# A recurrent-memory kernel: half of a streamed weight chunk made resident, paid for by a single output-tail buffer and a new schedule for the tail's heads

## Chip, cores, metric

One core of one Trainium2 chip. The metric is the device time of one execution in microseconds (us). The views of the profile name the engines PE (TensorE; PEld are its weight loads), DVE (VectorE), ACT (ScalarE), POOL (GpSimd) and SP (SyncE).

## The reference, cut to what matters

The program computes two unrelated things and lays them side by side. Part A (a long convolution by FFT) takes the first 470 us or so and the change does not touch it. Part B is a recurrence over 64 segments of 32 rows:

```python
mem = mem0                                     # 8 rows
for s in range(64):
    h = concat([mem, x[32 * s:32 * s + 32]])   # 40 rows
    q, k, v = h @ Wq, h @ Wk, h @ Wv           # 1024 -> 32 heads x 128 each
    p = softmax(where(mask, q @ k.T * scale, -1e9))
    o = (p @ v) @ Wo                           # 4096 -> 1024
    mem = o[:8]                                # the next segment needs this
    outs.append(o[8:])
```

`Wq`, `Wk`, `Wv` and `Wo` are 32 MB in bfloat16, and every segment needs all of them. They do not all fit on chip.

## The kernel before

The weights are 64 chunks of [128, 2048] bfloat16, 512 KB each. 43 stay on chip; 21 are streamed. Two of the streamed ones are kept in free accumulator columns after segment 0 ("kept"), so each segment loads 19 chunks from HBM through a ring of six slots. A slot is refilled when TensorE has used its chunk:

```python
STREAM = (0, 1, 3, 7, 11, 15, 21, 23, 25, 29, 33, 36, 40, 43, 46, 49, 51, 53, 59, 60, 62)
KEPT = {18: "A", 6: "B"}          # order_s[18] is place 59, order_s[6] is place 21
RING = 6

def fetch():                       # the next load, into a slot that has come free
    if loads:
        s, ch = loads.pop(0)
        live[s, ch] = k, t = slot()
        nc.sync.dma_start(t[:], stream_src(ch))

def done(ch):                      # after the last matmul that reads this chunk
    if ch in streamed:
        ...
        free.append(live.pop((now[0], ch))[0])
        ...
        if nxt in kept and s > 0:
            unkeep(s, kept[nxt])   # the freed slot takes the kept chunk back: no load here
        else:
            fetch()
```

A segment's places are: 0-7 K projection of head group 0 (`k0`), 8-15 Q, 16-23 K and 24-31 Q of group 1, 32-47 V, 48-63 the output projection (`out_proj`, two heads a chunk).

32 rows per segment (24 new ones and the 8 memory rows) go through the main path. The last 8 rows of a segment, the *tail*, have their attention computed there too, but their output projection is gathered over a pair of segments: `OTB` holds the tail's attention outputs of both, and the class `Tail` multiplies them by `Wo` head by head, 32 heads per pair. I call the first segment of a pair *even* (`j == 0`) and the second *odd*.

```python
class Tail:
    def __init__(self, OTB, b, acc=None):
        ...
        nc.vector.memset(self.acc, 0.0)            # columns of the accumulator tile SB
    def head(self, h, w): ...                      # 4 small matmuls; the 32nd calls store()
    def run(self, n): ...                          # n heads whose Wo chunk is resident
    def store(self):
        YB = one.tile([128, 256], BF, tag="QT", name="YB")   # QT0, QT1 and OT use this buffer too
        nc.vector.tensor_copy(YB[:], self.acc)
        for dq in range(4):
            nc.gpsimd.dma_start(<8 output rows of both segments>, YB[32 * dq:32 * dq + W, :])

# one segment, cut
k0 = Proj(0, 0).run().evac()
q0 = Proj(1, 0).run(4); KT0 = keys(0); last_queries(0); ...
k1 = Proj(0, 1).run(4)
QT0 = one.tile([128, 4, 4, 32], BF, tag="QT", name="QT")
nc.vector.tensor_copy(QT0[:], transposes(q0))
k1 = k1.run(4).evac()
scores(0, QT0, KT0)
...
out_proj(range(0, 5), OT0); attend(1, PT1, V1); OT1 = evac_o(1)
out_proj(range(5, 8), OT0)
out_proj(range(8, 16), OT1)        # tail heads of streamed chunks run inside, INLINE says in which segment
Y = one.tile([128, 256], BF, tag="PT", name="Y")
nc.scalar.copy(Y[:], yacc[:, 0:256])
if j == NB - 1 and not last:
    tail = Tail(OTB, b)
if tail is not None and not last:
    tail.run(TURN[0])              # 6 heads while ScalarE copies Y
if not last:
    fill_mem(pend[s + 1][0], Y)    # transposes of Y into the next segment's input
nc.gpsimd.dma_start(<output rows of segment s>, Y[:])
if tail is not None and not last:
    tail.run(TURN[1])              # 4 heads while VectorE copies the memory rows
```

The last lines are the *turn*: the next segment cannot start before the memory rows have gone from `Y` into its input.

Of the kernel before, what the change touches and what calls it, by code (L numbers as in the profile page):

```python
# [9 lines left out]
BF = mybir.dt.bfloat16  # L10
F32 = mybir.dt.float32
# [11 lines left out]
KEPT = {18: "A", 6: "B"}  # L23
TURN = (6, 4)
INLINE = {1: 0, 3: 1, 5: 0, 11: 1, 12: 0, 14: 1}
N2, N3 = 12, 19
# [358 lines left out]
def b_kernel(ctx: ExitStack, tc, x, mem0, Wq, Wk, Wv, Wo, outb, n_seg, run_a):  # L385
    nc = tc.nc
    SEG = 32
    NX = 24
    NB = 2
# [9 lines left out]
    order = []  # L399
# [7 lines left out]
    streamed = set()  # L407
# [4 lines left out]
    own = {mg: [ch for ch in resident if ch[0] < 3 and (ch[0], ch[2]) == mg] for mg in groups}  # L412
# [8 lines left out]
    def dram_chunk(ch):  # L421
        m, a, g = ch
        return Wo_v[a] if m == 3 else W_v[m][a, g]
# [4 lines left out]
    def stream_src(ch):  # L428
        return WS[ring_order.index(ch), :, 0:2048]
# [186 lines left out]
    one = ctx.enter_context(tc.tile_pool(name="b_one", bufs=1, side="right", reuse_waits="tile"))  # L616
    two = ctx.enter_context(tc.tile_pool(name="b_two", bufs=2, side="right", reuse_waits="tile"))
    ps_acc = ctx.enter_context(tc.tile_pool(name="b_ps_acc", bufs=2, space=PSUM))
# [15 lines left out]
    tacc = SB[:, 200:456]  # L634
# [14 lines left out]
    def slot():  # L649
        k = free.pop(0)  # L650
        t = ring.tile([128, 2048], BF, tag=f"wring{k}", name="wring")
        return k, t

    def fetch():
        if loads:
            s, ch = loads.pop(0)
            live[s, ch] = k, t = slot()
            nc.sync.dma_start(t[:], stream_src(ch))

# [12 lines left out]
    def pieces(ch):  # L672
        if ch in res:
            return [(0, 2048, res[ch])]
        t = live[now[0], ch][1]
        if kept.get(ch) == "B" and now[0] > 0:
            return [(0, 768, WB[:]), (768, 2048, t[:, 768:2048])]
        return [(0, 2048, t[:])]
# [7 lines left out]
    def done(ch):  # L686
        if ch in streamed:
# [7 lines left out]
            else:  # L695
                fetch()

    P_pad = one.tile([128, 5, 64], BF, name="P_pad")
    nc.vector.memset(P_pad[:], 0.0)

# [17 lines left out]
    with tc.manual_schedule():  # L718
# [17 lines left out]
        class Tail:  # L736


            def __init__(self, OTB, b, acc=None):
                self.OTB, self.b, self.acc = OTB, b, tacc if acc is None else acc  # L740
                self.seeded = acc is None
                self.left = list(range(32))
                nc.vector.memset(self.acc, 0.0)  # L743

            def head(self, h, w):
                g, c, i = h // 16, (h % 16) // 4, h % 4
                first = len(self.left) == 32
                self.left.remove(h)
                for dq in range(4):
                    o = (h % 2) * 1024 + dq * 256  # L750
                    for x, y, r in columns(w, o, o + 256):
                        nc.tensor.matmul(self.acc[32 * dq:32 * dq + W, x - o:y - o],  # L752
                                         lhsT=self.OTB[:, c, 4 * g + i, :], rhs=r,
                                         start=first and not self.seeded, stop=not self.left,
                                         skip_group_check=True, tile_position=(0, 32 * dq))
                if not self.left:
                    self.store()
# [12 lines left out]

        OTB = tail = own = None
        for s in range(n_seg):
# [60 lines left out]

            def softmax_a():
                mx = two.tile([128, 5], F32, tag="mx", name="mx")
                nc.vector.tensor_reduce(out=mx[:], in_=S, op=ALU.max, axis=AX.X)  # L836
                nc.vector.tensor_tensor(out=S, in0=S, in1=mx[:].unsqueeze(2).to_broadcast([128, 5, 40]),
                                        op=ALU.subtract)
                nc.scalar.activation(S, S, ACT.Exp, scale=scale)

            def softmax_b():
                ssum = two.tile([128, 5], F32, tag="ssum", name="ssum")
                nc.vector.tensor_reduce(out=ssum[:], in_=S, op=ALU.add, axis=AX.X)  # L843
# [38 lines left out]
            def out_proj(hps, OT):  # L882
                for hp in hps:
                    ch = (3, hp, 0)
                    w = pieces(ch)
                    for hh in range(2):
                        h = 2 * hp + hh
                        g, c, i = h // 16, (h % 16) // 4, h % 4
                        for dq in range(4):
                            o = hh * 1024 + dq * 256  # L890
                            for x, y, r in columns(w, o, o + 256):
                                nc.tensor.matmul(yacc[32 * dq:32 * dq + 32, x - o:y - o], lhsT=OT[:, c, i, :],  # L892
                                                 rhs=r, start=(h == 0 and x == o), stop=(h == 31),
                                                 tile_position=(0, 32 * dq))
                    if tail is not None and 2 * hp in tail.left and (ch in streamed or last):
                        if last or INLINE[hp] == j:
                            tail.head(2 * hp, w)
                            tail.head(2 * hp + 1, w)
                    if own is not None and ch in streamed:
                        own.head(2 * hp, w)  # L900
                        own.head(2 * hp + 1, w)
                    done(ch)

            k0 = Proj(0, 0).run().evac()
            q0 = Proj(1, 0).run(4)
# [8 lines left out]
            scores(0, QT0, KT0)  # L914
            softmax_a()
            q1 = Proj(1, 1).run(4)
            KT1 = keys(1)
            last_queries(1)
            nc.scalar.copy(KT1[:, :, :, 0:32], transposes(k1))
            PT0 = softmax_b()  # L920
            q1 = q1.run(4).evac()
# [4 lines left out]
            scores(1, QT1, KT1)  # L926
            softmax_a()
            pv1 = Proj(2, 1).run(4)
            if j == 0:
                OTB_new = one.tile([128, 4, 8, 8 * NB], BF, tag=f"OTB{b % 2}", name="OTB")  # L930
                OTB = OTB_new
            attend(0, PT0, V0)
            OT0 = evac_o(0)
            PT1 = softmax_b()
            pv1.run(4)
# [3 lines left out]
            yacc = ps_acc.tile([128, 512], F32, tag="acc", name="yacc")  # L939
            if last:  # L940
                own = Tail(OTB, b, ps_acc.tile([128, 512], F32, tag="acc", name="own_acc")[:, 0:256])
            out_proj(range(0, 5), OT0)
# [5 lines left out]
            nc.scalar.copy(Y[:], yacc[:, 0:256])  # L948
            if j == NB - 1 and not last:
                tail = Tail(OTB, b)  # L950
            if tail is not None and not last:
                tail.run(TURN[0])
            if not last:
                fill_mem(pend[s + 1][0], Y)
            nc.gpsimd.dma_start(bass.AP(outb.tensor, outb.offset + SEG * s * 2048, [[256, 4], [2048, 32], [1, 256]]), Y[:])
            if tail is not None and not last:
                tail.run(TURN[1])
            if last:
                own.run(32)

# [69 lines left out]
```

## Time and profile before

Median 2198.11 us of 3 runs (2195.46 to 2198.48). What matters:

| read from | value |
|---|---|
| pair of segments, from the copies of the memory rows | 53.63 us (even 26.31, odd 27.37) |
| lost DMA time per pair | 0.63 us |
| TensorE's waits for landing chunks, per pair | 2.4 us in the even, 3.6 us in the odd segment |
| QT0 copied, after the start of an even segment | 6.99 us |

A segment starts with the copy of the memory rows into its input; times "after the turn" count from there. "Lost DMA time" I worked out from the DMA packets of the trace: in each step of 0.05 us between segments 2 and 62, 16 less the packets in flight (0 where more than 16 are in flight), summed, divided by 16 and by the 30 pairs.

The page's slices (40 equal parts of the span, left to right): the granted TensorE clock in tenths, the busy share of the DMA engines in tenths, and what they moved.

```profile
span 2198.0 us, 81500 instructions
PEclk9889997879999999999999999999999999999999
DMA  9989989899999999999999999999999999999997
GB/s 322 345 291 342 318 238 325 275 346 390 386 380 378 381 374 390 385 378 395 391 392 395 391 393 393 392 397 365 396 392 387 394 390 376 388 392 388 390 385 273
q1 hardware_dynamic: 263592, 738.36, 89.0%
```

From the tenth slice on this is part B: DMA at "9" and 365 to 397 GB/s up to the last slice. The last line is the hardware queue: packets, MB, share of the engines.

Two groups of the page (matmuls of the projections from a streamed chunk, `wring`, and from a resident one, `Wres`): busy us, mean ns of one, and then the idle us before them:

```profile
L806 PE MATMUL acc<-wring,rec 128*32 128x512 bf16 (+1 forms) x3777 | 374.7, 385 | 136.0 <-DMA wring<-WS 122.1
L806 PE MATMUL acc<-Wres,rec 128*32 128x512 bf16 x4864 | 394.9, 383 | 1.5 <-issue 1.4
```

And from the view of waits from 500 us on (who waited for whom: us in total, times, longest):

```profile
PE acc L806 <- DMA wring<-WS: 119.4, 271, 2.0
PE yacc L892 <- DMA wring<-WS: 55.5, 105, 1.6
PE SB L827 <- DVE QT L912: 1.3, 2, 0.7
POOL out_dram L767 <- DVE YB L765: 212.9, 29, 16.2
DVE QT L912 <- DMA out_dram<-YB: 1.7, 1, 1.7
```

TensorE waits for streamed chunks and not for resident ones, and hardly ever for QT (twice, 1.3 us in all). The tail's store (YB) waits in 29 of 32 cases for its own copy, and QT, which shares its buffer, waited for the store once, 1.7 us.

### The profile page before, as it was taken

What the parts mean: (1) busy time and instruction counts of PE and PEld (TensorE: products, weight loads), DVE (VectorE), ACT (ScalarE), POOL (GpSimd) and SP (SyncE); (2) the same over time, 40 slices, a digit from 0 to 9 for tenths busy, and PEclk for the clock granted to TensorE, in tenths of its full rate; (3) what the DMA queues carried; (4) which work ended last, traced back from release to release, by engine and by line L of the source; (5) the groups of instructions that cost most, each with busy time, mean ns of one, the idle gap of its engine ahead of it and who ended that gap; (6) DMA issues with size and microseconds to landing.
All of it is one profiled execution on the core that took longest, in us unless ns stands there. A gap on an engine that the chain in (4) does not pass through costs nothing. (4 is left out here: it accounts for less than half of the span.)

```text
span 2198.0 us, 81500 instructions
## 1 busy us (share of the span) xinstructions
PE 1721.9 (78%) x35607; PEld 927.7 (42%) x35636; DVE 884.2 (40%) x2702; ACT 638.6 (29%) x1118; POOL 412.2 (19%) x1103
## 2 busy tenths in 40 slices
PE   4679975957777788878888888887887878888886
PEld 2233332424444444444444444444444444444444
DVE  8827853123333333333333333333333333333332
ACT  5845530112222222222222222222222222222222
POOL 5004331001111112111111111111111211211111
PEclk9889997879999999999999999999999999999999
DMA  9989989899999999999999999999999999999997
GB/s 322 345 291 342 318 238 325 275 346 390 386 380 378 381 374 390 385 378 395 391 392 395 391 393 393 392 397 365 396 392 387 394 390 376 388 392 388 390 385 273
DMA packets 294286, 807.80 MB, mean 368 GB/s; under 512 B 84940, under 2 KB 84972, under 8 KB 293927
## 3 DMA queue, kind: packets, MB, share of 16 engines
q1 hardware_dynamic: 263592, 738.36, 89.0%
q0 software_dynamic: 23536, 50.51, 6.8%
q10 hardware_dynamic: 6800, 13.72, 1.7%
q8 instruction: 279, 4.57, 0.9%
q14 instruction: 79, 0.65, 0.1%
HBM read 743.06 MB, written 62.39 MB: 366 GB/s over the span
## 5 line engine op out<-in xcount | busy, mean ns | idle before, releaser
L806 PEld LDWEIGHTS <-rec 128*32 128x32 bf16 x12351 | 324.2, 96 | 471.6 <-issue 255.0
L806 PE MATMUL acc<-wring,rec 128*32 128x512 bf16 (+1 forms) x3777 | 374.7, 385 | 136.0 <-DMA wring<-WS 122.1
L815 ACT CAST qkv_sb<-acc 128x512 bf16<-128x512 f32 x384 | 224.8, 585 | 676.2 <-PE acc L806 645.7
L806 PE MATMUL acc<-Wres,rec 128*32 128x512 bf16 x4864 | 394.9, 383 | 1.5 <-issue 1.4
L892 PEld LDWEIGHTS <-OT 128*32 128x32 bf16 x8192 | 217.8, 96 | 178.1 <-issue 151.6
L892 PE MATMUL yacc<-Wlate,OT 128*32 128x256 bf16 x5120 | 221.8, 274 | 13.0 <-issue 11.9
L892 PE MATMUL yacc<-wring,OT 128*32 128x256 bf16 x3072 | 153.9, 276 | 98.5 <-DMA wring<-WS 59.0
L806 PE MATMUL acc<-Wmid,rec 128*32 128x512 bf16 x3072 | 226.1, 383 | 0.5 <-issue 0.5
L752 PEld LDWEIGHTS <-OTB 128*16 128x16 bf16 x4096 | 104.5, 89 | 103.9 <-issue 94.0
L878 ACT CAST OT<-OTp 128x512 bf16<-128x512 f32 x128 | 74.9, 585 | 241.4 <-PE OTp L870 241.3
L707 POOL DMA_DIRECT2D rec<-REC x64 | 37.4, 584 | 566.6 <-issue 268.9
L908 DVE COPY KT<-tps 128x512 bf16<-128x512 bf16 x64 | 27.2, 424 | 289.1 <-PE tps L821 289.1
L879 DVE CAST OTB<-OTp 128x128 bf16<-128x128 f32 x128 | 37.3, 291 | 258.6 <-ACT OT L878 258.6
L647 DVE TENSOR_SCALAR wring<-OTp 128x384 int32<-128x384 int32 x126 | 112.2, 890 | 61.5 <-PE acc L806 54.2
L752 PE MATMUL SB<-Wlate,OTB 128*16 128x256 bf16 x2480 | 98.0, 277 | 35.4 <-DVE SB L743 19.3
L782 POOL COPY KT<-rec 128x128 bf16<-128x128 bf16 x128 | 38.6, 302 | 439.2 <-PE SB L830 430.9
L836 DVE TENSOR_REDUCE mx<-SB 128x5 f32<-128x200 f32 x128 | 47.1, 368 | 182.8 <-PE SB L830 182.8
L767 POOL DMA_DIRECT2D out_dram<-YB x128 | 73.1, 578 | 236.4 <-DVE YB L765 212.9
L752 PE MATMUL SB<-wring,OTB 128*16 128x256 bf16 x1488 | 78.8, 274 | 36.5 <-DVE SB L731 30.8
L821 PE MATMUL tps<-ident,qkv_sb 128*128 128x128 bf16 x1024 | 101.2, 221 | 7.8 <-DVE wring L647 0.2
L821 PEld LDWEIGHTS <-qkv_sb 128*128 128x128 bf16 x1024 | 62.7, 97 | 104.7 <-ACT qkv_sb L815 64.4
L556 PE MATMUL kb_ps<-XBT,pw 128*128 128x512 bf16 x314 | 87.7, 400 | 9.3 <-ACT XBT L512 7.6
(214 smaller groups left out, 2300.8 us busy)
## 6 DMA issues: line engine op xcount, KB each, us to landing
wring<-WS SPq DMA_DIRECT2D x1218, 512.0 KB, 7.3
rec<-REC POOLq DMA_DIRECT2D x64, 192.0 KB, 6.0
SK<-s_sb SPq DMA_DIRECT2D x16, 512.0 KB, 4.8
SU<-s_sb SPq DMA_DIRECT2D x16, 512.0 KB, 4.6
Ug<-SU SPq DMA_DIRECT2D x32, 256.0 KB, 6.1
Kg<-SK ACTq DMA_DIRECT2D x32, 256.0 KB, 5.5
REC<-stage SPq DMA_DIRECT2D x4, 2048.0 KB, 15.2
SZ<-zs SPq DMA_DIRECT2D x31, 256.0 KB, 3.0
```

Source lines behind the costliest of these rows:

```text
L556: nc.tensor.matmul(ps[:], lhsT=ws[kc][:, hl * 128:(hl + 1) * 128], rhs=XBT[:, kc].rearrange("p s t -> p (s t)"), start=(kc == 0), stop=(kc ...
L647: nc.vector.tensor_scalar(out=dst, in0=src, scalar1=0, scalar2=None, op0=ALU.bitwise_or)
L707: nc.gpsimd.dma_start(rec[:], REC[:, s, :])
L752: nc.tensor.matmul(self.acc[32 * dq:32 * dq + W, x - o:y - o], lhsT=self.OTB[:, c, 4 * g + i, :], rhs=r, start=first and not self.seeded, ...
L767: nc.gpsimd.dma_start(bass.AP(outb.tensor, outb.offset + (SEG * NB * self.b + NX) * 2048 + 256 * dq, [[2048 * SEG, NB], [2048, 8], [1, 256 ...
L782: nc.gpsimd.tensor_copy(KT[:, :, :, 32:40], KBs[:, 128 * g:128 * g + 128].rearrange("p (c i t) -> p i c t", c=4, i=4))
L806: nc.tensor.matmul(self.acc[32 * c:32 * c + 32, x - 512 * c:y - 512 * c], lhsT=hT[:, kc, :], rhs=r, start=(kc == 0 and x == 512 * c), stop ...
L815: nc.scalar.copy(sb[:], self.acc[:])
L821: nc.tensor.transpose(tp[:, i * 128:(i + 1) * 128], sb[:, i * 128:(i + 1) * 128], ident[:])
L836: nc.vector.tensor_reduce(out=mx[:], in_=S, op=ALU.max, axis=AX.X)
L878: nc.scalar.copy(OT[:], o_view[:, :, :, 0:32])
L892: nc.tensor.matmul(yacc[32 * dq:32 * dq + 32, x - o:y - o], lhsT=OT[:, c, i, :], rhs=r, start=(h == 0 and x == o), stop=(h == 31), tile_po ...
```

## The change

The intent: stream fewer bytes. Half of the chunk at place 3 (the fourth of the first K projection) becomes resident, 2 KB per partition. The room comes from three places: `OTB` is single instead of double, the softmax tile `P_pad` lives in the shared buffers `QT` and `KT` (and its zeros are written anew each time, on GpSimd), and the statistics have one buffer instead of two. (The diff also takes out a separate path for the tail of the very last pair.) With one `OTB` the tail must be done before the next even segment overwrites it, so its heads are rescheduled: 12 heads of streamed chunks in the odd segment's own output projection, 10 in the odd turn, 10 between the chunks of the next even segment's first K projection.

```diff
-TURN = (6, 4)
-INLINE = {1: 0, 3: 1, 5: 0, 11: 1, 12: 0, 14: 1}
+TURN = (4, 6)
+HALF = 3
...
+    half = order[HALF]
+    WH = one.tile([128, 1024], BF, name="WH")
+    nc.gpsimd.dma_start(WH[:], dram_chunk(half)[:, 0:1024])
     def fetch():
         ...
-            nc.sync.dma_start(t[:], stream_src(ch))
+            c = slice(1024 if ch == half else 0, 2048)
+            nc.sync.dma_start(t[:, c], stream_src(ch)[:, c])
...
+            def softmax_a(g):
+                P_pad = one.tile([128, 5, 64], BF, tag="KT" if g else "QT", name="P_pad")
+                nc.gpsimd.memset(P_pad[:, 0:4, 32:64], 0.0)
...
-                    if tail is not None and 2 * hp in tail.left and (ch in streamed or last):
-                        if last or INLINE[hp] == j:
-                            ...
+                    if j == NB - 1 and ch in streamed:
+                        tail.head(2 * hp, w)
+                        tail.head(2 * hp + 1, w)
...
-            k0 = Proj(0, 0).run().evac()
+            k0 = Proj(0, 0)
+            for n in (3, 3, 32, 0):
+                k0.run(2)
+                more_tail(n)           # tail.run(n) if j == 0; the 32nd head calls store()
+            k0 = k0.evac()
...
+            if j == NB - 1:
+                tail = Tail(OTB, b)    # now right after softmax_a(0)
...
-                OTB_new = one.tile([128, 4, 8, 8 * NB], BF, tag=f"OTB{b % 2}", name="OTB")
+                OTB = one.tile([128, 4, 8, 8 * NB], BF, tag="OTB", name="OTB")
...
-            if tail is not None and not last:
+            if j == NB - 1:
                 tail.run(TURN[0])
...
-            if tail is not None and not last:
-                tail.run(TURN[1])
+            if j == NB - 1:
+                tail.run(32 if last else TURN[1])
```

`store()`, which stood in the odd segment's output projection (at place 62), now runs at the third pause of the even segment's K projection, just before QT0 needs the same buffer.

More of the change, by code (lines that the diff above doesn't have):

```diff
@@ L616, in b_kernel @@
     one = ctx.enter_context(tc.tile_pool(name="b_one", bufs=1, side="right", reuse_waits="tile"))
-    two = ctx.enter_context(tc.tile_pool(name="b_two", bufs=2, side="right", reuse_waits="tile"))
+    two = ctx.enter_context(tc.tile_pool(name="b_two", bufs=1, side="right", reuse_waits="tile"))
     ps_acc = ctx.enter_context(tc.tile_pool(name="b_ps_acc", bufs=2, space=PSUM))
@@ L675, in pieces @@
         t = live[now[0], ch][1]
+        if ch == half:
+            return [(0, 1024, WH[:]), (1024, 2048, t[:, 1024:2048])]
         if kept.get(ch) == "B" and now[0] > 0:
@@ L696, in done @@
                 fetch()
-    P_pad = one.tile([128, 5, 64], BF, name="P_pad")
-    nc.vector.memset(P_pad[:], 0.0)
     QBm = one.tile([128, 4, 4, 32], BF, name="QBm")
@@ L736, in b_kernel, with __init__ @@
         class Tail:
-            def __init__(self, OTB, b, acc=None):
-                self.OTB, self.b, self.acc = OTB, b, tacc if acc is None else acc
-                self.seeded = acc is None
+            def __init__(self, OTB, b):
+                self.OTB, self.b, self.acc = OTB, b, tacc
                 self.left = list(range(32))
@@ L746, in head @@
                 g, c, i = h // 16, (h % 16) // 4, h % 4
-                first = len(self.left) == 32
                 self.left.remove(h)
@@ L753, in head @@
                                          lhsT=self.OTB[:, c, 4 * g + i, :], rhs=r,
-                                         start=first and not self.seeded, stop=not self.left,
+                                         start=False, stop=not self.left,
                                          skip_group_check=True, tile_position=(0, 32 * dq))
@@ L769, in store @@
                                 [[2048 * SEG, NB], [2048, 8], [1, 256]]), YB[32 * dq:32 * dq + W, :])
-        OTB = tail = own = None
+        OTB = tail = None
         for s in range(n_seg):
@@ L832, in scores @@
                                          tile_position=(0, 32 * c))
-            def softmax_a():
+            def softmax_a(g):
+                P_pad = one.tile([128, 5, 64], BF, tag="KT" if g else "QT", name="P_pad")
+                nc.gpsimd.memset(P_pad[:, 0:4, 32:64], 0.0)
                 mx = two.tile([128, 5], F32, tag="mx", name="mx")
@@ L839, in softmax_a, with softmax_b @@
                 nc.scalar.activation(S, S, ACT.Exp, scale=scale)
-            def softmax_b():
-                ssum = two.tile([128, 5], F32, tag="ssum", name="ssum")
+                return P_pad
+            def softmax_b(P_pad):
+                ssum = two.tile([128, 5], F32, tag="mx", name="ssum")
                 nc.vector.tensor_reduce(out=ssum[:], in_=S, op=ALU.add, axis=AX.X)
@@ L894, in out_proj, with more_tail @@
                                                  tile_position=(0, 32 * dq))
-                    if tail is not None and 2 * hp in tail.left and (ch in streamed or last):
-                        if last or INLINE[hp] == j:
-                            tail.head(2 * hp, w)
-                            tail.head(2 * hp + 1, w)
-                    if own is not None and ch in streamed:
-                        own.head(2 * hp, w)
-                        own.head(2 * hp + 1, w)
-                    done(ch)
-            k0 = Proj(0, 0).run().evac()
+                    if j == NB - 1 and ch in streamed:
+                        tail.head(2 * hp, w)
+                        tail.head(2 * hp + 1, w)
+                    done(ch)
+            def more_tail(n):
+                if tail is not None and j == 0:
+                    tail.run(n)
+            k0 = Proj(0, 0)
[3 more added lines that the diff above has]
+            k0 = k0.evac()
             q0 = Proj(1, 0).run(4)
@@ L914, in b_kernel @@
             scores(0, QT0, KT0)
-            softmax_a()
+            P0 = softmax_a(0)
+            if j == NB - 1:
+                tail = Tail(OTB, b)
             q1 = Proj(1, 1).run(4)
@@ L919, in b_kernel @@
             nc.scalar.copy(KT1[:, :, :, 0:32], transposes(k1))
-            PT0 = softmax_b()
+            PT0 = softmax_b(P0)
             q1 = q1.run(4).evac()
@@ L926, in b_kernel @@
             scores(1, QT1, KT1)
-            softmax_a()
+            P1 = softmax_a(1)
             pv1 = Proj(2, 1).run(4)
             if j == 0:
-                OTB_new = one.tile([128, 4, 8, 8 * NB], BF, tag=f"OTB{b % 2}", name="OTB")
-                OTB = OTB_new
+                OTB = one.tile([128, 4, 8, 8 * NB], BF, tag="OTB", name="OTB")
             attend(0, PT0, V0)
             OT0 = evac_o(0)
-            PT1 = softmax_b()
+            PT1 = softmax_b(P1)
             pv1.run(4)
@@ L939, in b_kernel @@
             yacc = ps_acc.tile([128, 512], F32, tag="acc", name="yacc")
-            if last:
-                own = Tail(OTB, b, ps_acc.tile([128, 512], F32, tag="acc", name="own_acc")[:, 0:256])
             out_proj(range(0, 5), OT0)
@@ L948, in b_kernel @@
             nc.scalar.copy(Y[:], yacc[:, 0:256])
-            if j == NB - 1 and not last:
-                tail = Tail(OTB, b)
-            if tail is not None and not last:
+            if j == NB - 1:
                 tail.run(TURN[0])
@@ L955, in b_kernel @@
             nc.gpsimd.dma_start(bass.AP(outb.tensor, outb.offset + SEG * s * 2048, [[256, 4], [2048, 32], [1, 256]]), Y[:])
-            if tail is not None and not last:
-                tail.run(TURN[1])
-            if last:
-                own.run(32)
+            if j == NB - 1:
+                tail.run(32 if last else TURN[1])
 @with_exitstack
```

## The prediction

> **What bounds the kernel now.** From about 470 us on, the kernel runs 64 dependent segments; a pair of them takes 53.63 us (times of the copies of the recurrent rows into the next input). The page's slices show DMA at "9" throughout, 380-395 GB/s. Folding the DMA packets over the pairs, the 16 engines are busy all the time but for dips to 94-98% at the turn between segments, 0.63 us of engine time per pair. Each segment loads 19 chunks of 512 KB, landing 1.30 us apart (128 packets of 4 KB, median 162 ns, over 16 engines: 1.296 us). TensorE idles for landing chunks 3.6 us (odd) and 2.4 us (even segment) of each pair, by the waits. So the DMA engines bind, the first case of the Trainium skill's "Perfetto Trace Analysis", section What "DMA-bound" means; the trace agrees.
>
> **What the change does.**
> 1. Half of one chunk becomes resident: 256 KB less of about 10.3 MB per segment. The same 128 packets become 2 KB long; 2 KB packets take 84 ns in this trace, so 128 x 78 ns / 16 = 0.62 us less DMA per segment. The split falls on a matmul boundary: TensorE's instruction count is unchanged.
> 2. The tail's 32 heads per pair cost TensorE the same (0.11 us each). Now 10 run in the odd turn, 10 in the next first K projection (+1.1 us there), 12 in the odd output projection (+0.66 us); the even segment's end loses 16 (-1.8 us). The clearing of the tail's accumulator leaves the turn, where TensorE waited 0.65 us per pair for it. Mostly hidden under the DMA bound.
> 3. A new wait: the tail's rows are stored about 3 us into the even segment, from the buffer that QT0 needs. The store's four issues take 0.58 us each and land after 5.1 us, so QT0, now at 7.0 us, should come at about 10 us, scores(0) with it: a TensorE stall of roughly 2 us. About four chunks are outstanding then (over 4 us of DMA work), so the queue should mostly not drain; I charge at most 0.3 us per pair.
> 4. P_pad's memset (GpSimd) is far ahead of its use. The half-filled slot makes the queue 0.65 us shallower at the turn; engines still ran at 99% with two loads outstanding, 81% with one.
>
> **Sum.** 64 x 0.62 = 40 us saved in the stream, less a few us for dips and the QT0 wait: about 37 us, 1.7%. Predicted 2161 us, 8 in 10 between 2149 and 2178. Faster by over 2% (below 2154) 0.2, within 2% 0.78, slower 0.02.
>
> **What would show each step.** Right: the hardware queue's bytes fall by about 16.6 MB (738.4 to 722); the pair falls to 52.3-52.6 us; DMA stays at "9", GB/s unchanged; the wait for the accumulator's memset at the turn goes; even QT0 waits for the store, TensorE for QT, with little fall of the DMA share. Wrong: the pair falls by under 0.8 us while lost DMA time per pair rises well above 0.63 us (the chain through turn, tail heads and QT0 has become the limit), or 2 KB packets take clearly over 84 ns.
>
> **What would make it wrong.** The QT0 stall may drain the six-slot ring, and the shallower queue at the odd turn add to it: a third to a half of the saving is lost (2170-2180). Or the lighter even turn and the earlier memset remove most of the 0.63 us of dips: up to 15 us more (2148).

## The result, and the profile after

The changed kernel takes 2367.07 us (median of 4, 2364.12 to 2380.15) against 2196.84 us for the kernel before in the same rounds: ratio 1.0786, 95% interval 1.0744 to 1.0828. A ratio is the mean time of one kernel's runs over the mean of the other's in the same rounds, so it is not quite the ratio of the medians quoted. The prediction was 2161 us: wrong in sign, and far outside its range (2149 to 2178).

| per pair of segments | before | after |
|---|---|---|
| period | 53.63 us | 59.03 us |
| even, odd segment | 26.31, 27.37 | 31.19, 27.76 |
| TensorE waiting for QT0, even segment | 0.04 us | 5.07 us |
| lost DMA time | 0.63 us | 5.37 us |
| QT0 copied after the turn, even segment | 6.99 us | 13.70 us |

The same lines of the page:

```profile
span 2363.2 us, 82008 instructions
PEclk9899987799999999999998999999999999999898
DMA  9989799899999999999989999999999999999996
GB/s 334 338 289 346 265 317 303 275 384 348 350 340 348 346 340 343 344 339 342 338 328 340 350 350 343 349 351 338 337 348 346 349 346 339 340 344 341 329 346 250
q1 hardware_dynamic: 263592, 721.58, 83.5%
L808 PE MATMUL acc<-wring,rec 128*32 128x512 bf16 (+1 forms) x3649 | 405.5, 410 | 92.7 <-DMA wring<-WS 75.1
L808 PE MATMUL acc<-Wres,rec 128*32 128x512 bf16 x4864 | 448.1, 422 | 1.2 <-issue 1.0
```

The bytes fell exactly as planned (738.36 to 721.58 MB), and the digit for DMA stays "9", because a digit covers everything over 90%. But the rate fell from about 390 to about 345 GB/s. That row was the one to look at. And the matmuls from resident chunks, which wait for nobody, take 422 ns in place of 383.

The waits from 500 us on:

```profile
DVE QT L921 <- DMA out_dram<-YB: 192.0, 31, 8.3
PEld L829 <- DVE QT L921: 172.1, 31, 7.9
PE SB L829 <- DVE QT L921: 158.0, 31, 7.4
POOL out_dram L769 <- issue: 78.5, 18, 5.7
POOL out_dram L769 <- DMA out_dram<-Y: 75.4, 14, 6.6
PE acc L808 <- DMA wring<-WS: 71.9, 153, 2.0
PE yacc L897 <- DMA wring<-WS: 25.9, 60, 1.0
```

Read it from the bottom. TensorE waits *less* for chunks (98 us in place of 175). It now waits for QT0 (L829 is L827 of the kernel before), 31 times, once a pair. QT0 waits for the store of YB to land. And the store itself waits for the landing of `out_dram<-Y`, the output rows of the odd segment that has just ended, sent off at the turn (in 14 of the cases; in 18 the profile names nobody). The times of landing in the trace settle those 18: in all 31 pairs the store's first issue comes 0.65 to 0.72 us after that write of Y has landed.

A stretch of the timeline shows one such stall (start us, length, engine, line, what; in brackets the idle time before and who ended it). The segment began at 1112.3:

```profile
1112.18 0.73 POOL L961 DMA_DIRECT2D out_dram<-Y  x1 [8.78 <-ACT Y L956]
1115.42 0.42 DVE L767 CAST YB<-SB 128x256 bf16<-128x256 f32 x1 [2.97 <-PE SB L754]
1118.49 2.27 POOL L769 DMA_DIRECT2D out_dram<-YB  x4 [5.05 <-issue]
1125.18 0.42 DVE L921 COPY QT<-tps 128x512 bf16<-128x512 bf16 x1 [5.53 <-DMA out_dram<-YB]
1125.66 0.22 PE L829 MATMUL SB<-KT,QT 128*32 128x40 bf16 x4 [4.59 <-DVE QT L921]
1126.75 1.07 PE L808 MATMUL acc<-Wres,rec 128*32 128x512 bf16 x8
```

YB is ready at 1115.8, but its writes are issued at 1118.5, when Y's write, issued at 1112.2, has landed (at 1117.84). They land at about 1125, QT0 follows, then TensorE. The eight matmuls of the last line take 1.07 us; eight such take 0.60 to 0.62 us in the kernel before.

Table by stage for the same segment: start to stall, the stall, and after it (the columns to look at are PE busy, then the last three, granted clock, DMA share, GB/s):

```profile
core 0: us, PE busy (x) PEld busy (x) DVE busy (x) ACT busy (x) POOL busy (x), PEclk, DMA share, GB/s
1112.00:1121.00 9.00, 8.32 (x171) 4.58 (x171) 1.93 (x5) 1.17 (x2) 3.77 (x8) 1.00 1.00 371
1121.00:1125.50 4.50, 0.06 (x4) 0.00 (x0) 0.32 (x1) 0.59 (x1) 0.65 (x5) 0.83 0.98 364
1125.50:1131.00 5.50, 5.34 (x80) 2.08 (x84) 3.01 (x14) 1.50 (x3) 1.04 (x6) 0.52 0.50 159
```

During the stall itself DMA still runs at 0.98: the loads that were outstanding cover it. It is *after* the stall that DMA falls to half (0.50): TensorE has freed no slots for 4.5 us and now runs at half clock (0.52), so it frees them slowly. The other pairs show the same: of the 5.37 us of lost DMA time per pair, about 3.9 lie 13 to 25 us after the turn of the even segment (before: none), and at most one load was outstanding for 5.6 us per pair (before: 0.15). Lost time is not all of the loss, though: the 4 KB packets also took longer on the mean (174.9 ns in place of 168.4; the median fell from 162 to 159), which is 1.9 us of DMA time per pair. Why they did, no run here shows.

### The profile page after: what moved, and what is told of

It is laid out like the page before. It is cut to its first block, busy times and chain, and to the rows that moved or that the text cites. A ratio compares the mean times of both kernels' runs of the same rounds, so it can differ in the third digit from the quotient of the medians.

```text
span 2363.2 us, 82008 instructions
## 1 busy us (share of the span) xinstructions
PE 1774.6 (75%) x35636; PEld 937.2 (40%) x35636; DVE 883.9 (37%) x2701; ACT 638.9 (27%) x1118; POOL 437.6 (19%) x1232
## 3 DMA queue, kind: packets, MB, share of 16 engines
q1 hardware_dynamic: 263592, 721.58, 83.5%
## 4 chain that ended last, share of the span: by engine, by line
DMA 42%; PE 33%; issue 10%; DVE 6%; ACT 3%; POOL 3%; SPq 1%; DVEq 0%; ACTq 0%; POOLq 0%
DMA wring<-WS 25%; PE acc L808 15%; DMA out_dram<-YB 7%; DMA out_dram<-Y 4%; PE kb_ps L556 3%; PE yacc L897 3%; PE SB L754 3%; DVE wring L647 3%; PE vb_ps L598 2%; POOL out_dram L769 2%; PE tps L823 2%; DMA zt<-SZ 1%; ACT s_sb L210 1%; ACT OT L883 1%; DMA SU<-s_sb 1%
## 5 line engine op out<-in xcount | busy, mean ns | idle before, releaser
L808 PEld LDWEIGHTS <-rec 128*32 128x32 bf16 x12351 | 333.0, 101 | 425.2 <-issue 232.1
L808 PE MATMUL acc<-wring,rec 128*32 128x512 bf16 (+1 forms) x3649 | 405.5, 410 | 92.7 <-DMA wring<-WS 75.1
L808 PE MATMUL acc<-Wres,rec 128*32 128x512 bf16 x4864 | 448.1, 422 | 1.2 <-issue 1.0
L897 PE MATMUL yacc<-Wlate,OT 128*32 128x256 bf16 x5120 | 228.4, 276 | 24.8 <-issue 24.5
L808 PE MATMUL acc<-Wmid,rec 128*32 128x512 bf16 x3072 | 233.4, 391 | 4.1 <-issue 3.6
L829 PE MATMUL SB<-KT,QT 128*32 128x40 bf16 x2048 | 46.8, 186 | 158.0 <-DVE QT L921 158.0
L838 POOL MEMSET P_pad<- 128x128 bf16 x128 | 26.3, 205 | 733.3 <-PE SB L832 733.3
L961 POOL DMA_DIRECT2D out_dram<-Y x64 | 46.1, 721 | 482.8 <-ACT Y L956 467.9
L823 PE MATMUL tps<-ident,qkv_sb 128*128 128x128 bf16 x1024 | 107.4, 231 | 10.5 <-issue 2.9
L829 PEld LDWEIGHTS <-QT 128*32 128x32 bf16 x2048 | 39.1, 97 | 190.0 <-DVE QT L921 172.1
```

Of the source, the lines that this page charges most:

```text
L808: nc.tensor.matmul(self.acc[32 * c:32 * c + 32, x - 512 * c:y - 512 * c], lhsT=hT[:, kc, :], rhs=r, start=(kc == 0 and x == 512 * c), stop ...
L823: nc.tensor.transpose(tp[:, i * 128:(i + 1) * 128], sb[:, i * 128:(i + 1) * 128], ident[:])
L829: nc.tensor.matmul(S[32 * c:32 * c + 32, i, :], lhsT=QT[:, i, c, :], rhs=KT[:, i, c, :], start=False, stop=False, skip_group_check=True, t ...
L897: nc.tensor.matmul(yacc[32 * dq:32 * dq + 32, x - o:y - o], lhsT=OT[:, c, i, :], rhs=r, start=(h == 0 and x == o), stop=(h == 31), tile_po ...
```

## The experiments

Theories, as they came up: **A**, the late store holds QT0's buffer; **B**, its rival, the half-filled slot and the heads in the K projection starve the queue whatever the store does; **C**, the empty even turn drops TensorE's clock; **D**, the place of the ten heads is the cost; **E**, the half chunk is the wrong load to halve; **F**, bytes do not matter, the chain through the turn sets the period.

### 1. The store moved to the end of the even segment (correct)

```diff
-                if not self.left:
+                if not self.left and last:
                     self.store()
...
-            out_proj(range(8, 16), OT1)
+            out_proj(range(8, 14), OT1)
+            if tail is not None and j == 0:
+                tail.store()
+            out_proj(range(14, 16), OT1)
```

Everything else is as changed. The accumulator is not needed before the next odd segment, so the store can wait.

> The changed kernel with one edit: the tail's store (the copy to YB and its four writes) is moved from the pause in the even segment's first K projection to the end of the same even segment's output projection, where the kernel before had it; QT0 then no longer waits for the store. Theory A (the late store holds QT0's buffer, TensorE stalls 5.07 us per pair, the load queue runs dry): QT0 of even segments returns from 13.7 us to 7-8 us, lost DMA time per pair from 5.37 us to under 1 us, the pair to 52.3-52.8 us, and the whole to 2155-2170 us, faster than before by 1.2-1.9%. Theory B (the half-filled ring slot and ten tail heads inside the first K projection starve the queue whatever the store does): it stays above 2280 us.

(One slip in this text: the kernel before had its store at the end of the odd segment. The call was put at the end of the even one.)

Measured: 2204.31 us, ratio 1.0031 (1.0001 to 1.0061). QT0 of even segments is back at 8.30 us, and its wait for the store is gone from the waits. The view of the tile YB, before the edit (the changed kernel) and after it:

```profile
L767 DVE CAST YB<-SB x32: 424/425/426, 526.9 to 2353.2; 128x256 bf16<-128x256 f32 x32
  DVE QT L921: 192.0, 31
  POOL out_dram L769: 75.1, 15
```

```profile
L767 DVE CAST YB<-SB x32: 414/415/425, 548.4 to 2197.5; 128x256 bf16<-128x256 f32 x32
  POOL out_dram L769: 149.4, 31
```

The lines under the first are who waited for YB. QT has left the list.

So Theory A holds for most of the loss: 7.55 points of ratio, about 166 us, hang on this one call's place. But the expectation of 2155 to 2170 us failed: 40 us that should have been saved are not there, and lost DMA time per pair is 1.59 us, still above the 0.63 us before.

### 2. No resident half, the store late as changed (correct)

```diff
-    half = order[HALF]
-    WH = one.tile([128, 1024], BF, name="WH")
-    nc.gpsimd.dma_start(WH[:], dram_chunk(half)[:, 0:1024])
+    half = None
```

> The changed kernel without the resident half: the chunk is streamed whole, everything else as changed. Theory A: the stall on QT0 is the same, so the time stays near the changed kernel's, 2355-2405 us (up to 1.3 us per pair more DMA work, which may partly fill the stall). Theory B (the shallower queue of the half slot does it): it falls most of the way back, to 2200-2260 us.

Measured: 2379.69 us, ratio 1.0838 (1.0803 to 1.0874), TensorE's wait for QT0 4.98 us per pair. The half-filled slot is out as the cause of the large loss: without the half the stall is just as long. The heads in the K projection, the other part of Theory B, are out by experiment 1, which keeps them.

### 3. No resident half, and the store at the end (correct)

The edits of experiments 1 and 2 together:

```diff
+    half = None                        # WH and its load removed
...
-                if not self.left:
+                if not self.left and last:
                     self.store()
...
-            out_proj(range(8, 16), OT1)
+            out_proj(range(8, 14), OT1)
+            if tail is not None and j == 0:
+                tail.store()
+            out_proj(range(14, 16), OT1)
```

> Both edits: no resident half, and the store at the end of the even segment. What is left of the change is the tail's new schedule, the single buffers and P_pad in the shared buffers. Theory A: within 0.7% of before, 2182-2212 us, and the difference to the run with the late store and the half is the half's own worth, 64 x 0.64 us = 41 us (2 KB packets took 86 ns on the mean in the changed kernel). Theory B: above 2240 us, because the heads in the first K projection remain.

Measured: 2221.76 us, ratio 1.0100 (1.0061 to 1.0139). It missed the range, by 10 us, on the slow side. The rescheduled tail costs about 1.0%, 22 us, by itself (with the single buffers and `P_pad` in the shared ones), where I had reckoned nothing. And the difference to experiment 1, on the same chip, is 0.7 points, 15 us: the half is worth 15 us there, give or take 11 us by the two intervals, and not 41.

The four runs cross the two edits, so each is measured twice: the store's place makes 7.55 points with the half and 7.38 without it, and the half 0.7 points with the late store and 0.5 with the early one.

### 4. The store written to a scratch tensor (wrong result in the tail's rows)

```diff
+    SCR = dram.tile([n_seg // NB, 4, W, 256], BF, name="SCR")
...
-                        bass.AP(outb.tensor, <the tail's output rows>), YB[32 * dq:32 * dq + W, :])
+                        SCR[self.b, dq].rearrange("(s r) d -> s r d", s=NB), YB[32 * dq:32 * dq + W, :])
```

Y's write covers all 32 rows of its segment, also the eight that the tail's store overwrites. So in the changed kernel the store has to wait until Y's write has landed. A scratch tensor has no such earlier write.

> The changed kernel with the tail's rows written to a scratch tensor, so that the store has no earlier write of the same output rows to wait for (the result is wrong on purpose in those rows). Theory A1 (the store waits for the landing of the segment's own output write, 5.9 us after the turn, which my prediction left out): the store's first issue comes at about 3.9 us instead of 6.3, its last landing at about 10.5-11.2 instead of 13.2, QT0 at 10.8-11.5 instead of 13.7, TensorE's stall falls from 5.07 to 2-3 us per pair, and the time to 2180-2290 us. What a stall of 2 us costs is then read off: my prediction charged 0.3 us per pair, which would be 2170-2180 us. Rival (the store's delay comes from elsewhere, as the queue of GpSimd): QT0 stays beyond 13 us and the time above 2350 us.

Measured: 2295.84 us, ratio 1.0434 (1.0391 to 1.0477), slightly over the expected range. QT0 is copied at 11.31 us, and TensorE waits 2.49 us per pair for it. The waits from 500 us on:

```profile
POOL SCR L770 <- DVE YB L768: 98.1, 32, 4.5
DVE QT L921 <- DMA SCR<-YB: 111.3, 30, 4.8
PE SB L829 <- DVE QT L921: 79.6, 30, 3.9
```

The store no longer waits for Y, only for its own copy: its first issue comes at 3.88 us (median) after the turn, in place of 6.24. This run has the stall that I predicted (about 2 us) and shows what such a stall costs: 4.03 points more than experiment 1, some 89 us over 32 pairs, 2.8 us per pair. I had charged 0.3.

### 5. TensorE kept busy through the stall (correct)

```diff
             k1 = k1.run(4).evac()
+            if tail is not None and j == 0:
+                for m in range(60):
+                    nc.tensor.matmul(OTp[:, m % 4, 0:160], lhsT=ident[:], rhs=WB[:, 0:160], start=True, stop=True,
+                                     skip_group_check=True)
             scores(0, QT0, KT0)
```

The changed kernel, store and half as they were, with dummy matmuls in the stall.

> The changed kernel as it is, with 60 dummy matmuls of 160 columns (about 4 us) in TensorE's stream before scores(0) of even segments, inside the stall on QT0, so that TensorE is not idle there (result correct, dummies unread). It splits the stall's cost in two: the stall itself, and the half clock after it (100% of the matmuls between 12 and 13 us at half clock in the changed kernel). If the clock carries a third of it: matmuls after the stall at 380 ns, the time falls from 2367 to 2290-2330 us. If the stall alone carries it: within 15 us of 2367.

Measured: 2334.99 us, ratio 1.0624 (1.0582 to 1.0666), just above the range. QT0 comes as late as before (13.94 us), but the matmuls between 13 and 15 us after the turn take 381 to 386 ns; in the changed kernel they took 601 to 611. So about 1.6 points, 36 us of the 173, went with the half clock after the stall. The dummies did not remove all of it: time at half clock after 497 us fell from 279 to 129 us, and experiment 1 has 69. Most of the loss stays: lost DMA time is still 4.80 us per pair.

### 6. Filler in the even turn (correct)

On top of experiment 1: in the even turn, from which the change took the heads, 40 and 24 small dummy matmuls stand where `tail.run(6)` and `tail.run(4)` stood.

```diff
+            def filler(n):
+                if j == 0 and not last:
+                    for m in range(n):
+                        for dq in range(4):
+                            nc.tensor.matmul(OTp[32 * dq:32 * dq + W, m % 4, 0:160], lhsT=ident[:, 0:W],
+                                             rhs=WB[:, 0:160], start=True, stop=True,
+                                             skip_group_check=True, tile_position=(0, 32 * dq))
...
                 tail.run(TURN[0])
+            filler(10)
...
                 tail.run(32 if last else TURN[1])
+            filler(6)
```

> The changed kernel with the late store, plus filler in the even segment's turn, where the change left TensorE without tail heads: 64 small matmuls on free accumulator columns, whose result nobody reads, in the two places where the tail's heads stood. Theory C (the empty turn lets TensorE's granted clock drop to one half, seen in 19-22% of the matmuls of the first 3 us of odd segments against 0% before, and that lengthens the chain that frees ring slots): the share at half clock falls to at most 5%, the time at half clock after 497 us from 69 us to under 40 us (before: 32 us), and the whole falls 8-25 us below the run with the late store. Rival D (the ten heads in the first K projection are the cost, the clock is a bystander): clock restored, time within 5 us of the run with the late store.

Measured: 2209.64 us, ratio 1.0052 (1.0025 to 1.0080). No gain. The time at half clock after 497 us fell from 69 to 47 us, not under 40, and odd segments became 0.3 us shorter (27.53 to 27.25), but even ones 0.4 us longer (26.49 to 26.89). The filler was probably longer than the wait that it filled. Inconclusive, and tried again below, shorter.

### 7. The ten heads moved to the first V projection (correct)

On top of experiment 1:

```diff
+            k0 = Proj(0, 0).run().evac()        # no heads in it
...
-            pv0 = Proj(2, 0).run(4)
+            pv0 = Proj(2, 0).run(2)
+            more_tail(3)
+            pv0.run(2)
+            more_tail(3)
...
-            V0 = pv0.run(4).evac()
+            pv0.run(2)
+            more_tail(32)
+            V0 = pv0.run(2).evac()
```

> The changed kernel with the late store, and with the ten heads moved out of the first K projection of the even segment to the first V projection, where TensorE waits for landing chunks. Theory D (the heads in the first K projection lengthen the stretch in which ring slots come free late: slot 11 of the even segment is freed at 8.9 us after the turn against 7.5 before): slot 11 comes at about 7.7 us, lost DMA time falls from 1.6 us per pair towards 0.8, and the time falls by 20-40 us to 2160-2185 us. Theory C alone: it stays within 8 us of the run with the late store.

Measured: 2216.43 us, ratio 1.0098 (1.0057 to 1.0140). The slot indeed comes earlier (7.67 us in place of 8.90), and it did not help: the kernel is slower than experiment 1 and lost DMA time rose to 1.81 us per pair. Theory D in this form falls.

### 8. The old schedule with a quarter resident at place 3 (correct)

The kernel before, with its own tail schedule and double `OTB`, `P_pad` in the shared buffers and single statistics buffers as in the change, and 512 columns of the same chunk resident. It separates the byte saving from the tail's schedule. Against the kernel before:

```diff
+HALF = 3
...
+    half = order[HALF]
+    WH = one.tile([128, 512], BF, name="WH")
+    nc.gpsimd.dma_start(WH[:], dram_chunk(half)[:, 0:512])
...
-            nc.sync.dma_start(t[:], stream_src(ch))
+            c = slice(512 if ch == half else 0, 2048)
+            nc.sync.dma_start(t[:, c], stream_src(ch)[:, c])
...
+            def softmax_a(g):
+                P_pad = one.tile([128, 5, 64], BF, tag="KT" if g else "QT", name="P_pad")
+                nc.gpsimd.memset(P_pad[:, 0:4, 32:64], 0.0)
```

> The kernel before, with its own tail schedule and its doubled output-tail buffer, and a quarter of the same chunk resident (1 KB per partition, which P_pad in shared buffers and single statistics buffers pay for). If the byte saving is worth what I reckoned (0.32 us per segment here) and P_pad in shared buffers is harmless: 20 us faster than before, 0.9% (0.6 to 1.1%). If the bytes are worth only what they gave between the runs with the late store (17 us for the half): 8 us, 0.4%. If P_pad in shared buffers costs: slower than before.

Measured: 2196.29 us, ratio 0.9988 (0.9952 to 1.0023). Together the saved bytes and `P_pad` in the shared buffers changed nothing that shows. No run moves `P_pad` alone, so a cost of it that cancels the saving is not ruled out by this run; and the interval leaves room for up to half of the 20 us. The trace speaks for the bytes being lost again: lost DMA time rose from 0.63 to 1.07 us per pair. Alone this run would fit Theory F as well; the next ones speak to that.

### 9 to 11. The resident part taken from place 43

Where do the saved bytes go? The DMA packets tell. In experiment 1 lost DMA time in odd segments, 24 to 28 us after the turn, is 0.51 us; before it was 0.06, without the half 0.15. That stretch is the gap before the turn: at place 53 the freed slot takes a kept chunk back instead of a load, and the next slot comes free only at place 59, 3.5 us later. The last load issued before that gap is place 3 of the next segment, the one that was halved. Place 43 lies in the V projection, where TensorE waits for each chunk and about four loads are outstanding.

```diff
-HALF = 3
+HALF = 43
```

This one line is the edit against experiment 1 (first run) and against experiment 8 (second run). The half, new schedule, store late:

> The changed kernel with the late store, and the resident half taken from another chunk: the twelfth load of the segment (place 43, in the second V projection), where TensorE waits for every landing, in place of the third load (place 3), which is in flight in the gap before the turn in which no slot comes free for 3.3-3.7 us. Theory E (halving the load that is in flight in that gap drains the queue there, so that the bytes saved return as lost DMA time, 1.59 us per pair against 0.63): lost time falls to about 0.8-1.0 us, the load after the gap is no longer starved (3.2 us from issue to landing in even segments rises to about 3.7), and the time is 20-40 us below the run with the late store and the half at place 3: 2160-2185 us. Theory F (the chain of work through the turn sets the period and bytes do not matter anywhere): within 8 us of that run, 2196-2212 us.

The quarter, old schedule:

> The kernel before with the resident quarter at place 43 instead of place 3. Theory E: 15-20 us faster than before, 0.7-0.9% (the quarter at place 3 gave 0.1%). Theory F: within 0.3% of before.

Experiment 1 again, on the same chip:

> The run with the late store again (half at place 3), on the same chip as the two above, so that the place of the half is compared within one call. Both theories: 2196-2210 us.

Measured, in the order above: 2194.79 us, ratio 0.9984 (0.9950 to 1.0017); 2181.04 us, ratio **0.9937 (0.9897 to 0.9978)**; 2195.29 us, ratio 0.9993 (0.9958 to 1.0028). The kernel before had a median of 2194.77 us.

In the old schedule the quarter at place 43 gives 0.6%, 14 us, of the 20 us that its bytes are worth by the packets' durations. That fits Theory E, and so do the traces (one each): lost DMA time is 0.78 us per pair with the quarter at place 43 and 1.07 with it at place 3. But the intervals of the two quarters (0.9952 to 1.0023 in one call, 0.9897 to 0.9978 in another) overlap a little, so the place is likely and not proven. In the new schedule the half at place 43 gives no more than the half at place 3. The stretch before the odd turn improved, 0.51 to 0.28 us of lost DMA time, but what even segments won (26.30 to 25.80 us) odd ones lost (27.33 to 27.99 us), and TensorE spent 104 us at half clock after 497 us, against 57 in the repeat of experiment 1. The first run thus met neither expectation (2160 to 2185 and 2196 to 2212 us), and the repeat of experiment 1 came out just under its own. So Theory E is right about the gap and not enough. Theory F loses with the quarter at place 43, whose interval lies below 1; its upper end, 0.9978, would still be within the 0.3% that Theory F allowed.

### 12 to 15. Splitting what the new schedule costs

With a shorter filler (24 and 12 matmuls), against experiment 6:

```diff
-            filler(10)
+            filler(6)
...
-            filler(6)
+            filler(3)
```

The runs with the half also have `HALF = 43`, those without it the edit of experiment 2, and those with heads in the V projection the edit of experiment 7. Half at 43, store late, filler:

> Late store, half at place 43, and a shorter filler in the even turn (24 and 12 small matmuls, about as long as the 6 and 4 heads that stood there; the first filler had 40 and 24 and lengthened the even segment by 0.4 us). The half at place 43 alone had 33-44% of the matmuls between 2 and 5 us of odd segments at half clock. If that half clock (theory C) is what keeps the half at place 43 from paying: half-clock share at most 5%, odd segments from 27.99 to 27.2-27.5 us, time 10-25 us below before, 2170-2185 us. If the clock does not matter: 2190-2200 us as without the filler.

The same, heads in the V projection:

> The same with the ten heads in the first V projection in place of the first K projection. If the ring slots freed late during the first K projection (theory D, lost DMA time of 0.20 us per pair between 10 and 16 us of even segments) are what is left of the schedule's cost: another 5-15 us faster than with the filler alone, 2160-2175 us. If not: within 5 us of it.

No half, store late, filler, heads in the V projection:

> No resident half, late store, filler in the even turn, heads in the first V projection: the new tail schedule with both of its suspected faults mended and no bytes saved. Without the mends it was 22 us (1.0%) slower than before. If clock and place of the heads are the whole of that: within 0.3% of before. If neither: still 0.8-1.2% slower.

No half, store late, filler, heads in the K projection as changed:

> No resident half, late store, filler in the even turn, heads in the first K projection: splits the 22 us between the clock and the place of the heads. Theory C alone: back to within 0.4% of before. Theory D alone: still 0.8% or more slower. Both: about half way, 0.5%.

| run | median us | ratio (95%) |
|---|---|---|
| half at 43, filler | 2187.27 | 0.9966 (0.9939-0.9993) |
| half at 43, filler, heads in V | 2206.31 | 1.0054 (1.0023-1.0085) |
| no half, filler, heads in V | 2217.54 | 1.0102 (1.0071-1.0132) |
| no half, filler | 2207.16 | 1.0044 (1.0020-1.0068) |

Heads in the V projection are worse than in the K projection in both comparisons, by 0.6 and 0.9 points on one chip, against the expectation that they would gain or cost nothing; why, the traces did not settle. With the filler, time at half clock after 497 us fell from 116 us (experiment 3) to 48, and the schedule's own cost from 1.0100 to 1.0044. That is the direction of Theory C, but the two are from different calls, the intervals overlap and the difference (0.56 points) is not much more than the 0.4 by which the repeat of experiment 1 moved: that the clock is half of the 22 us is not shown. About 10 us stay unexplained in any case. With the half at place 43, late store and filler the changed design is 0.3% faster than before (2187 us, between the two ranges expected). The lowest median of all is the old schedule with a quarter resident at place 43. The page of that run:

```profile
span 2180.0 us, 82005 instructions
GB/s 325 347 290 348 328 249 335 259 354 392 380 370 391 389 379 388 391 387 396 386 386 392 391 395 390 384 393 386 386 368 364 386 385 367 385 388 386 392 391 270
q1 hardware_dynamic: 263592, 729.97, 88.7%
```

Its rate is that of the kernel before with 8.39 MB less on the queue. So here fewer bytes at the same rate became less time.

## Why the prediction was wrong, point by point

- **What bounds the kernel: right, as a share, and badly used.** The loop was bound on the DMA engines, and the trace agreed with the Trainium skill's "Perfetto Trace Analysis", section What "DMA-bound" means. But TensorE idled for landing chunks only 6.0 us of the 53.63 us of a pair, and it alone frees the six slots, so its chain was close behind. I treated the DMA bound as slack for TensorE.
- **Step 1, 0.62 us less DMA per segment: right in the packets, wrong in the time.** 2 KB packets took 84 ns (median) as predicted and the queue moved 721.58 MB. The term "64 x 0.62 = 40 us saved" was mis-sized: experiments 1 and 3 put it at 15 us. The half was taken from the load that carries the queue over the gap before the turn, and part of the saving came back as lost DMA time (1.59 us per pair with the half, experiment 1, against 0.99 without it, experiment 3).
- **Step 2, the moved heads "mostly hidden under the DMA bound": wrong.** The new schedule costs 22 us by itself (experiment 3). The even turn lost its heads, and TensorE its clock there: time at half clock after 497 us is 116 us in experiment 3, 32 before and 48 with dummies in that turn. How much of the 22 us that is stays open; the measured ratios (1.0100 and 1.0044) would put it at about half, which is not clear of the noise between calls.
- **Step 3, the QT0 wait: the mechanism right, and both of its sizes wrong.** This is the step that failed the prediction. It said that QT0 "should come at about 10 us" with "a TensorE stall of roughly 2 us", and charged "at most 0.3 us per pair". QT0 came at 13.70 us and the stall was 5.07 us, because the store has to wait for the landing of the write of Y to the same rows. The Trainium skill's "DMA: Bandwidth & Descriptors", section Two DMAs through the same engine are not ordered, states why such a wait must stand there: the same queue or engine does not order two DMAs, so the issuing engine has to wait for the first one's semaphore before it issues one that depends on it (here a second write to the same rows). The prediction does not mention this wait. The trace agrees: the issue comes at a median of 6.24 us after the turn with the wait, 0.65 to 0.72 us after Y has landed, and experiment 4, which takes the wait away, issues at 3.88 and gets QT0 at 11.31. Second, even the 2.5 us stall costs 2.8 us per pair (experiment 4): outstanding loads do cover the stall itself, but afterwards the ring has to be refilled by a TensorE at half clock. The whole stall cost about its own length too: 7.55 points are 5.2 us per pair.
- **Step 4, P_pad in shared buffers: right as far as the runs go** (the quarters at place 3, ratio 0.9988, and at place 43, 0.9937, both have it; none has it alone).
- **"What would make it wrong"** named the QT0 stall and the odd turn, the right places, and gave them 2170 to 2180 us in place of 2367.

In ratio points the loss of 7.86 splits into 7.55 for the store's place (3.5 of them the wait for Y's landing; by a different cut, 1.6 the clock after the stall), 1.0 for the schedule, minus 0.7 for the half. These are differences of the same runs, so their sum is no check; the check is the crossed pair in experiment 3, 7.38 for the store's place without the half.

## What to carry to other kernels

When a copy or store moves to a new place, follow its buffer both ways: who must have left it, and who needs it next, and add every wait of the store's own issue (an earlier write to the same rows of the output counts) before giving the stall a length. In a loop where the compute engine frees the slots that loads go into, a stall is not covered by the loads in flight: DMA keeps running through it and then falls short while the ring refills, and here each stall cost about its whole length (2.8 us for 2.5, 5.2 us for 5.1), part of it through TensorE's clock. And before saving bytes in a DMA-bound loop, look where the queue is shallow: the runs here suggest, without proving it, that a load that carries the queue over a gap is the wrong one to shrink, and that one from a stretch in which the consumer waits for every landing is better.

## What the Trainium skill lacked or had wrong

- "TensorE: Matmul & The Clock Gate", What's actually happening, gives the cold state "after ≥1 idle window (~3.4µs)", and its section on oscillation warns of idle gaps over 3.4 us. Here half as much was enough: in experiment 1, between 600 and 2150 us, the clock went to half 15 times, each for 3.4 or 6.8 us, and in the 3.4 us before those, TensorE (matmuls and weight loads) had been idle for 1.8 us at the median, in gaps of at most 1.9 us. Cut the same stretch of all 17 traces into steps of 3.41 us, on the grid on which these records start: the 340 steps at whose end the clock fell were idle for at least 1.24 us, and none of the 7297 others that began at full clock was idle for over 2.0 us. So idle time adds up within a step, and about half a step of it is where the clock falls here. The length of the half-clock records and the two levels agree with the page.
- "DMA: Bandwidth & Descriptors" has no figure for how many loads must be in flight. With 512 KB loads the kernel before had on the mean 15.7 to 15.9 packets in flight (counted up to 16) with three or more loads outstanding, 15.5 with two and 13.1 with one, so slightly less at two than the 99% of the prediction; a load onto an idle queue took 0.94 us to its first packet and 2.9 us to its last (changed kernel).
- "Perfetto Trace Analysis", DMA Optimizations, calls DMAs under 2 KB costly. It gives no figure at the edge: for packets of exactly 2 KB (of a load of 256 KB) the changed kernel's trace shows 84 ns against 159 ns for 4 KB (medians), 6% more per byte.
- "Perfetto Trace Analysis", What "DMA-bound" means, does not say that bytes saved in such a loop can come back as lost DMA time: 15 us of 41 arrived for the half at place 3 (new schedule), 14 of 20 for the quarter at place 43 (old schedule), and nothing that shows of 20 for the quarter at place 3.
